# A six-layer cross network on one core: how the first group of x0 reaches TensorE, and who issues two small loads

## The chip, the core and the metric

The kernel runs on one core of a Trainium2 chip. The core has a matrix engine (TensorE, PE in the profile; its weight loads are listed as PEld), a vector engine (VectorE, DVE), a scalar engine (ScalarE, ACT), a general engine (GpSimd, POOL) and a synchronisation engine (SyncE, SP). Data comes from the chip's main memory by DMA; SP, ACT and GpSimd each can issue DMAs on a queue of their own. TensorE writes to the accumulation memory PSUM, which DVE and ACT read.

The metric is device time in microseconds (us), lower is better. "A us at 12.14" below means 12.14 us after the start of the profiled span.

## The reference

Six layers of a cross network, with B = 4096 rows, D = 416 columns, all in bf16:

```python
B, F, D, L = 4096, 26, 16, 6
Din = min(F * D, 1024)                 # 416
x0: (B, Din)   ws: (L, Din, Din)   bs: (L, Din)

def reference(x0, ws, bs):
    x = x0
    for l in range(ws.shape[0]):
        x = x0 * (x @ ws[l] + bs[l]) + x
    return x
```

## The kernel before

The kernel keeps x transposed on the core: columns of x on the 128 partitions, rows along the free axis. The 416 columns are three full planes of 128 (`NK = 3`) and a remainder of 32 (`R`). The planes are in `XM[0]` (x0) and `XM[1]`, `XM[2]` (the running x, by turns), the remainder in `XR[0]` to `XR[2]`, with four groups of rows stacked on the 128 partitions. The 4096 rows are two halves (`s`), each of four groups (`g`) of 512 rows (`CW`).

Layer weights are in `WM` (the 384 rows of the planes) and `WR` (the 32 rows of the remainder, four times on the partitions); `WD` is a block layout of the remainder-by-remainder weights, filled by GpSimd (`fill_wd`, L131). Biases arrive as rows in `bsb` and are transposed on TensorE into `bM` and `bR` (`bias_setup`, L146).

**The head.** SP issues transposing loads, one for each `(s, g)`, which bring 512 rows by 384 columns of x0 from memory straight into `XM[0]` (`load_x0t`, L76): first `(0,0)` and `(0,1)`, then WR of layer 0 (L88), then `(0,2)`, `(0,3)`, `(1,0)`, the remainder columns of s=1 (`xrem`, L85), and the last three of s=1; then the later layers' weights. ACT issues WM of layer 0 (L72), `bsb` (L102) and four loads of the remainder columns of s=0 into `xrig` (L81). ACT and GpSimd then copy WR's 32 rows to the other three strips (L110, L112). While nothing has landed, TensorE runs filler matmuls on a constant tile (`pe_filler`, L141: two of 256 columns, eight of 512, and one more of 512 that the built kernel puts with the others).

**The first layer** (`first_layer`, L208) for s=0: nine matmuls of g=0 (three output planes `m` by three input planes `k`, L214), four transposes of `xrig` (`x0_rem`, L157) whose result DVE copies to `XR[0]` and, with the strips exchanged, to `XRd` (L160); nine matmuls of g=1; eight row matmuls that add the remainder's share (L221); then g=2 and g=3 of each output plane, four more row matmuls, the remainder outputs (`mm_rem`: four of WD at L193, twelve of WM at L198) and the four transposes of s=1's remainder. ACT adds the bias out of PSUM (L165), DVE multiplies by x0 (L166) and adds x (L169). The same follows for s=1, without the transposes.

**Middle layers** run over pairs of tiles `(s, m)` (L181, L187), and **the last layer** swaps the operands, so that it comes out as plain rows, which SP stores.

Engines take their own instructions in order. Which order they stand in is decided by a scheduler when the kernel is built, except where `tc.keep_in_program_order` pins an instruction. PSUM has four slots of two banks (`tag="ps"`); a new tile waits until the one before it in its slot has been read.

In the built kernel, GpSimd's queue before is: constants, identity, zeroing WD, the WR copy, the four WD copies of layer 0, the copy of `xrem` into `xrig` (L134), the later WD copies.

Of the kernel before, what the change touches and what calls it, by code (L numbers as in the profile page):

```python
# [11 lines left out]
BF16 = mybir.dt.bfloat16  # L12
FP32 = mybir.dt.float32
# [3 lines left out]
def kernel(  # L17
# [7 lines left out]
    nc = tc.nc  # L25
    B, D = x0.shape
    L = ws.shape[0]
    P = 128
    NK = 3
    R = D - NK * P  # L30
    assert R == 32 and B == 4096 and D == 416 and L >= 2
    NS = 2
    NG = 4
    CW = 512
# [5 lines left out]
    big = ctx.enter_context(tc.tile_pool(name="big", bufs=1))  # L40
    tpool = ctx.enter_context(tc.tile_pool(name="tpool", bufs=6))
    opool = ctx.enter_context(tc.tile_pool(name="opool", bufs=10))
    psum = ctx.enter_context(tc.tile_pool(name="psum", bufs=4, space=bass.MemoryType.PSUM))

    x0_v = x0.rearrange("(bt p) d -> p bt d", p=P)
    out_v = out.rearrange("(bt p) d -> p bt d", p=P)

    ident = const.tile([P, P], BF16)
    dz = const.tile([P, 2], FP32)
    warm = const.tile([P, CW], BF16)  # L50
    ones = const.tile([P, P], BF16)
    WM = const.tile([P, L, NK, D], BF16)
    WR = const.tile([P, L, D], BF16)
    WD = const.tile([P, L, NG, R], BF16)
    bsb = const.tile([L, D], BF16)
    bLr = const.tile([P, D], BF16)
    bM = const.tile([P, NK, L], FP32)
    bR = const.tile([P, L], FP32)
    X0rows = big.tile([P, NBT, D], BF16)
    XLrows = big.tile([P, NBT, D], BF16)  # L60
    scrR = [big.tile([P, 4, P], BF16, name=f"scrR{s}") for s in range(NS)]
    xrem = big.tile([P, 16, R], BF16)
    xrig = big.tile([P, NS, 4, P], BF16)
    XRd = big.tile([P, NS * CW], BF16)
    XM = [big.tile([P, NK, B], BF16, name=f"XM{i}") for i in range(3)]
    XR = [big.tile([P, NS * CW], BF16, name=f"XR{i}") for i in range(3)]

    def col0(s, g):
        return SW * s + CW * g

    def load_wm(eng, l):
        eng.dma_start(WM[:, l], ws[l, 0:NK * P, :].rearrange("(k p) n -> p k n", p=P))  # L72

    def load_x0t(s, g):
        c0 = col0(s, g)
        nc.sync.dma_start_transpose(out=XM[0][:, :, c0:c0 + CW], in_=x0[c0:c0 + CW, 0:NK * P])  # L76

    def load_xrem0():
        with nc.allow_non_contiguous_dma(reason="64B row segments"):
            for i in range(4):  # L80
                nc.scalar.dma_start(xrig[:, 0, i, :].rearrange("p (g r) -> p g r", g=NG), x0_v[:, i:16:4, NK * P:D])  # L81

    def load_xrem1():
        with nc.allow_non_contiguous_dma(reason="64B row segments"):
            nc.sync.dma_start(xrem[:], x0_v[:, 16:32, NK * P:D])  # L85

    def load_wr0():
        nc.sync.dma_start(WR[0:R, 0, :], ws[0, NK * P:D, :])  # L88

    def load_wr(eng, g, l0, l1):  # L90
        eng.dma_start(WR[32 * g:32 * g + 32, l0:l1, :], ws[l0:l1, NK * P:D, :].rearrange("l r n -> r l n"))
# [2 lines left out]
        nc.vector.memset(warm[:, 2 * P * a:2 * P * a + 2 * P], 0.5)  # L94
    nc.vector.memset(dz[:], 0.0)
    make_identity(nc, ident[:])
    nc.gpsimd.memset(ones[:], 1.0)
    nc.gpsimd.memset(WD[:], 0.0)

    load_x0t(0, 0)  # L100
    load_wm(nc.scalar, 0)
    nc.scalar.dma_start(bsb[:], bs[:, :])  # L102
    load_x0t(0, 1)
    load_xrem0()
    load_wr0()
    nc.scalar.activation(dz[:, 1:2], dz[:, 0:1], ACT.Identity, bias=dz[:, 0:1], scale=1.0)  # L106
    for g in range(1, NG):
        dst, src = WR[32 * g:32 * g + 32, 0, :], WR[0:R, 0, :]
        if g < NG - 1:
            nc.scalar.copy(dst, src)  # L110
        else:
            nc.gpsimd.tensor_copy(dst, src)  # L112
    for g in range(2, NG):
        load_x0t(0, g)
    load_x0t(1, 0)
    load_xrem1()
    for g in range(1, NG):
# [11 lines left out]
    def fill_wd(l0, l1):  # L129
        for g in range(NG):  # L130
            nc.gpsimd.tensor_copy(WD[32 * g:32 * g + 32, l0:l1, g, :], WR[32 * g:32 * g + 32, l0:l1, NK * P:D])  # L131

    fill_wd(0, 1)
    nc.gpsimd.tensor_copy(xrig[:, 1].rearrange("p i (g r) -> p i g r", g=NG), xrem[:].rearrange("p (g i) r -> p i g r", g=NG))  # L134
    fill_wd(1, L)

    wps = psum.tile([P, CW], FP32, tag="ps", name="wps")

    def pe_filler(n, cols):
        for i in range(n):  # L140
            nc.tensor.matmul(wps[:, 0:cols], lhsT=warm[:, 0:P], rhs=warm[:, 0:cols], start=True, stop=True)  # L141

    pe_filler(2, 2 * P)
    pe_filler(8, CW)

    def bias_setup():  # L146
        pb = psum.tile([P, 4, 8], BF16, tag="ps", name="pb")
        for m in range(NK):
            nc.tensor.transpose(pb[:, m, 0:L], bsb[0:L, 128 * m:128 * m + 128], ident[0:L, 0:L])
        for g in range(NG):  # L150
            nc.tensor.transpose(pb[32 * g:32 * g + 32, 3, 0:L], bsb[0:L, NK * P:D], ident[0:L, 0:L], tile_position=(0, 32 * g))  # L151
        nc.vector.tensor_copy(bM[:], pb[:, 0:NK, 0:L])  # L152
        nc.vector.tensor_copy(bR[:], pb[:, 3, 0:L])

    def x0_rem(s, tpr):
        for i in range(4):
            nc.tensor.transpose(tpr[:, 128 * i:128 * i + 128], xrig[:, s, i, :], ident[:])  # L157
        for dst, src in ((slice(0, P), slice(0, P)), (slice(64, P), slice(0, 64)), (slice(0, 64), slice(64, P))):
            to = XR[0] if dst == src else XRd
            nc.vector.tensor_copy(to[dst, CW * s:CW * s + CW], tpr[src])  # L160

    def ew_main(l, s, m, h, pt, cur, nxt, pin=False):
        c0 = col0(s, 2 * h)
        t = tpool.tile([P, 2 * CW], BF16, name="t")
        nc.scalar.activation(t[:], pt[:].rearrange("p a b -> p (a b)"), ACT.Identity, bias=bM[:, m, l:l + 1], scale=1.0)  # L165
        prod = nc.vector.tensor_tensor(out=t[:], in0=t[:], in1=XM[0][:, m, c0:c0 + 2 * CW], op=ALU.mult)  # L166
        if pin:
            tc.keep_in_program_order(prod)
        nc.vector.tensor_tensor(out=nxt[:, m, c0:c0 + 2 * CW], in0=t[:], in1=cur[:, m, c0:c0 + 2 * CW], op=ALU.add)  # L169
# [21 lines left out]
    def mm_rem(l, s, pr, cur, curR):  # L191
        for g in range(NG):
            nc.tensor.matmul(pr[32 * g:32 * g + 32, :], lhsT=WD[:, l, g, :], rhs=curR[:, CW * s:CW * s + CW],  # L193
                             start=True, stop=False, tile_position=(0, 32 * g))
        for k in range(NK):
            for g in range(NG):
                c0 = col0(s, g)
                nc.tensor.matmul(pr[32 * g:32 * g + 32, :], lhsT=WM[:, l, k, NK * P:D], rhs=cur[:, k, c0:c0 + CW],  # L198
                      start=False, stop=(k == NK - 1), tile_position=(0, 32 * g))
# [8 lines left out]
    def first_layer(s):  # L208
        cur, curR, nxt, nxtR = XM[0], XR[0], XM[1], XR[1]

        def full(pt, m, h, gl, after_row):
            c0 = col0(s, 2 * h + gl)
            for k in range(NK):
                nc.tensor.matmul(pt[:, gl, :], lhsT=WM[:, 0, k, 128 * m:128 * m + 128], rhs=cur[:, k, c0:c0 + CW],  # L214
                                 start=(k == 0 and not after_row), stop=(k == NK - 1 and after_row))

        def row(pt, m, h, opens):
            for gl in range(2):
                rg = 32 * ((2 * h + gl) ^ (2 if m == 1 else 0))
                src = XRd if m == 1 else curR  # L220
                nc.tensor.matmul(pt[:, gl, :], lhsT=WR[rg:rg + 32, 0, 128 * m:128 * m + 128],  # L221
                                 rhs=src[rg:rg + 32, CW * s:CW * s + CW],
                                 start=opens, stop=not opens, tile_position=(rg, 0))

        def ph(m):
            return psum.tile([P, 2, CW], FP32, tag="ps", name=f"ph{m}")

        pa = [ph(m) for m in range(NK)]
        if s == 0:
            for m in range(NK):  # L230
                full(pa[m], m, 0, 0, False)
            tp0 = psum.tile([P, CW], BF16, tag="ps", name="tpr")
            x0_rem(0, tp0[:])
            for m in range(NK):
                full(pa[m], m, 0, 1, False)
        else:
            for m in range(NK):
                for gl in range(2):
                    full(pa[m], m, 0, gl, False)
        pb = [ph(0)]  # L240
        row(pa[0], 0, 0, False)
        row(pb[0], 0, 1, True)
        row(pa[2], 2, 0, False)
        row(pa[1], 1, 0, False)
        for m in range(NK):
            ew_main(0, s, m, 0, pa[m], cur, nxt)
        for m in range(NK):
            if m:
                pb.append(ph(m))
            for gl in range(2):  # L250
                full(pb[m], m, 1, gl, m == 0)
        row(pb[1], 1, 1, False)
        row(pb[2], 2, 1, False)
        pr = psum.tile([P, 2, CW], FP32, tag="ps", name="pr")
        mm_rem(0, s, pr[:, 0, :], cur, curR)
        if s == 0:
            x0_rem(1, pr[:, 1, :].bitcast(BF16)[:, 0:CW])
        for m in range(NK):
            ew_main(0, s, m, 1, pb[m], cur, nxt, pin=(s == 0))
        ew_rem(0, s, pr[:, 0, :], curR, nxtR)  # L260

    bias_setup()
    pe_filler(1, CW)
    for s in range(NS):
        first_layer(s)

# [14 lines left out]
    cur, curR = XM[1], XR[1]  # L281
    for l in range(1, LL):
# [30 lines left out]
        cur, curR = nxt, nxtR  # L313

    l = LL
# [97 lines left out]
```

## Time and profile before

| What | Value |
|---|---|
| Median of 3 runs | 130.95 us (130.82 to 131.1) |
| The profiled execution's own time | 130.71 us |
| Its span | 128.9 us |
| TensorE clock granted in it | 0.998 |
| Read from memory / written | 6.15 MB / 3.41 MB |
| SP's transposing loads of x0 | 8, median 4.9 us from issue to landing |
| xrig's four loads on ACT | 32 KB each, median 4.1 us |
| xrem's load on SP | 128 KB, 4.3 us |

Times in the profile come from one execution; the span runs from the first to the last instruction, and the run's time is 1.8 us longer. The row below gives the busy share of the DMA engines in 40 equal slices of 3.2 us, in tenths:

```profile
DMA  3999999999990000000000000000297999995754
```

So the loads fill the first 12 slices, the turning of x back into rows and the stores fill the last dozen. The page also names the costliest groups: line, engine, operation, output and inputs, count | busy us, mean ns | idle before. Three of them, which show what the middle of the kernel is made of:

```profile
L181 PE MATMUL pt<-XM,WM 128*32 128x512 bf16 x1152 | 65.2, 379 | 0.0
L165 ACT ACTIVATE t<-pt,bM 128x1024 bf16<-128x1024 f32 x48 | 49.6, 1115 | 18.3 <-PE pt L187 18.3
L166 DVE TENSOR_TENSOR t<-t,XM 128x1024 bf16<-128x1024 bf16 x60 | 41.4, 690 | 5.3 <-ACT t L165 5.3
```

A matmul's 379 ns is the time from its start to its modelled end; they overlap, so their count times their pitch, not times 379 ns, is the time that TensorE needs.

### The profile page before, as it was taken

Reading aid. Unit: us, or ns where it says so; the run is one execution under the profiler, and the core shown is the slowest. Engines: PE = TensorE matmul, PEld = TensorE weight load, DVE = VectorE, ACT = ScalarE, POOL = GpSimd, SP = SyncE. Lnnn points to the kernel's source line nnn. Section 1 sums busy time; section 2 is a strip of 40 time slices with the busy share of each in tenths; the row PEclk is TensorE's granted clock in tenths of the full one; section 3 lists DMA queues with packets and bytes.
Section 4 is the critical chain, followed back from the end, with each engine's and each line's share of the span. In section 5 each row is a group of like instructions: output and inputs, shape, how many; then the busy total and the mean of one; then the engine's idle time right before and its main releaser. Section 6 shows DMA issues by size and latency. Waiting matters only on the chain.

```text
span 128.9 us, 3973 instructions
## 1 busy us (share of the span) xinstructions
PE 123.1 (96%) x1690; PEld 54.9 (43%) x1690; DVE 107.1 (83%) x197; ACT 86.9 (67%) x99; POOL 5.9 (5%) x18
## 2 busy tenths in 40 slices
PE   6999999999999999999999999999999999999960
PEld 2343443354444444444444444444444445445420
DVE  1032979999999898989898989898989899898991
ACT  0426783987848577848668848668847896569670
POOL 4022200600000000000000000000000000000000
PEclk9999999999999999999999999999999999999999
DMA  3999999999990000000000000000297999995754
GB/s 106 237 203 217 170 158 260 247 328 333 336 299 11 5 0 8 0 0 5 0 5 0 5 0 5 0 5 0 42 166 164 123 219 178 187 323 188 231 179 139
DMA packets 42102, 16.37 MB, mean 127 GB/s; under 512 B 30906, under 2 KB 42084, under 8 KB 42084
## 3 DMA queue, kind: packets, MB, share of 16 engines
q1 hardware_dynamic: 39416, 15.56, 54.6%
q10 hardware_dynamic: 2668, 0.56, 2.3%
q8 instruction: 13, 0.21, 0.7%
q14 instruction: 5, 0.04, 0.1%
HBM read 6.15 MB, written 3.41 MB: 74 GB/s over the span
## 4 chain that ended last, share of the span: by engine, by line
PE 80%; DMA 8%; DVE 5%; issue 2%; SPq 1%; ACT 1%; DVEq 0%
PE pt L181 49%; PE ph L214 9%; DMA XM<-in_x_dram 8%; PE py L327 8%; PE pt L187 5%; PE pr L198 5%; DVE t L355 3%; DVE o L344 2%; PE pr L193 2%; SPq L76 1%; PE py L333 1%; PE ph L221 1%; PE py L336 1%; ACT t L354 1%; PE pr L157 0%
## 5 line engine op out<-in xcount | busy, mean ns | idle before, releaser
L181 PE MATMUL pt<-XM,WM 128*32 128x512 bf16 x1152 | 65.2, 379 | 0.0
L165 ACT ACTIVATE t<-pt,bM 128x1024 bf16<-128x1024 f32 x48 | 49.6, 1115 | 18.3 <-PE pt L187 18.3
L166 DVE TENSOR_TENSOR t<-t,XM 128x1024 bf16<-128x1024 bf16 x60 | 41.4, 690 | 5.3 <-ACT t L165 5.3
L169 DVE TENSOR_TENSOR XM<-t,XM 128x1024 bf16<-128x1024 bf16 x60 | 41.8, 696 | 3.4
L181 PEld LDWEIGHTS <-WM 128*32 128x32 bf16 x1152 | 29.7, 97 | 33.8 <-issue 5.1
L354 ACT CAST t<-py 128x416 bf16<-128x416 f32 (+1 forms) x23 | 14.8, 642 | 4.8 <-PE py L327 2.1
L327 PE MATMUL py<-WM,XM 128*128 128x416 bf16 x96 | 17.7, 340 | 0.0
L214 PE MATMUL ph<-XM,WM 128*128 128x512 bf16 x72 | 16.5, 379 | 0.1
L165 ACT ACTIVATE t<-ph,bM 128x1024 bf16<-128x1024 f32 x12 | 12.5, 1114 | 4.4 <-PE ph L221 4.4
L327 PEld LDWEIGHTS <-XM 128*128 128x128 bf16 x96 | 9.0, 98 | 8.5 <-issue 1.4
L355 DVE TENSOR_TENSOR t<-t,X0rows 128x416 bf16<-128x416 bf16 (+1 forms) x23 | 10.4, 454 | 1.2 <-ACT t L354 1.2
L214 PEld LDWEIGHTS <-WM 128*128 128x128 bf16 x72 | 6.8, 98 | 8.6 <-issue 1.3
L344 DVE TENSOR_TENSOR o<-t,XLrows 128x416 bf16<-128x416 bf16 (+1 forms) x23 | 10.3, 451 | 0.0
L173 ACT ACTIVATE t<-pr,bR 128x512 bf16<-128x512 f32 x10 | 6.4, 684 | 2.7 <-PE pr L198 2.1
L198 PE MATMUL pr<-XM,WM 128*32 128x512 bf16 x120 | 8.2, 379 | 0.0
L187 PE MATMUL pt<-XR,WR 32*128 32x512 bf16 x96 | 7.3, 379 | 0.0
L141 PE MATMUL wps<-warm 128*128 128x512 bf16 (+1 forms) x11 | 4.4, 593 | 1.2 <-DVE warm L94 1.2
L175 DVE TENSOR_TENSOR XR<-t,XR 128x512 bf16<-128x512 bf16 x10 | 4.2, 423 | 0.7
L198 PEld LDWEIGHTS <-WM 128*32 128x32 bf16 x120 | 3.2, 97 | 3.1
L106 ACT ACT_TABLE_LOAD x1 | 1.3, 1283 | 4.3 <-DMA WM<-in_ws_dram 4.3
L174 DVE TENSOR_TENSOR t<-t,XR 128x512 bf16<-128x512 bf16 x10 | 4.2, 418 | 0.0
L152 DVE CAST bM<-pb 128x18 f32<-128x18 bf16 x1 | 0.2, 177 | 4.6 <-PE pb L151 4.6
(39 smaller groups left out, 33.6 us busy)
## 6 DMA issues: line engine op xcount, KB each, us to landing
X0rows<-in_x_dram SPq DMA_DIRECT2D x4, 832.0 KB, 11.6
out_dram<-o SPq DMA_DIRECT2D x9, 208.0 KB, 2.4
WM<-in_ws_dram SPq DMA_DIRECT2D x5, 312.0 KB
out_dram<-o SPq DMA_DIRECT2D x13, 104.0 KB, 1.7
WR<-in_ws_dram SPq DMA_DIRECT2D x4, 130.0 KB, 4.1
WM<-in_ws_dram ACTq DMA_DIRECT2D x1, 312.0 KB
XM<-in_x_dram SPq DMA_TRANSPOSE x8, 4.9
xrig<-in_x_dram ACTq DMA_DIRECT2D x4, 32.0 KB, 4.1
```

The source lines that it names most:

```text
L165: nc.scalar.activation(t[:], pt[:].rearrange("p a b -> p (a b)"), ACT.Identity, bias=bM[:, m, l:l + 1], scale=1.0)
L166: prod = nc.vector.tensor_tensor(out=t[:], in0=t[:], in1=XM[0][:, m, c0:c0 + 2 * CW], op=ALU.mult)
L169: nc.vector.tensor_tensor(out=nxt[:, m, c0:c0 + 2 * CW], in0=t[:], in1=cur[:, m, c0:c0 + 2 * CW], op=ALU.add)
L173: nc.scalar.activation(tr[:, 0:CW], pr, ACT.Identity, bias=bR[:, l:l + 1], scale=1.0)
L181: nc.tensor.matmul(pts[g // 2][32 * q:32 * q + 32, g % 2, :], lhsT=WM[:, l, k, 128 * m + 32 * q:128 * m + 32 * q + 32], rhs=cur[:, k, c0:c ...
L187: nc.tensor.matmul(pts[g // 2][:, g % 2, :], lhsT=WR[32 * g:32 * g + 32, l, 128 * m:128 * m + 128], rhs=curR[32 * g:32 * g + 32, CW * s:CW ...
L198: nc.tensor.matmul(pr[32 * g:32 * g + 32, :], lhsT=WM[:, l, k, NK * P:D], rhs=cur[:, k, c0:c0 + CW], start=False, stop=(k == NK - 1), tile ...
L214: nc.tensor.matmul(pt[:, gl, :], lhsT=WM[:, 0, k, 128 * m:128 * m + 128], rhs=cur[:, k, c0:c0 + CW], start=(k == 0 and not after_row), sto ...
L327: nc.tensor.matmul(py[:, 0:D], lhsT=cur[:, k, q_cols(q, g)], rhs=WM[:, l, k, :], start=((not closes) and k == 0), stop=(closes and k == NK ...
L344: tc.keep_in_program_order(nc.vector.tensor_tensor(out=o, in0=t, in1=xl, op=ALU.add))
L354: nc.scalar.copy(tv, src)
L355: tc.keep_in_program_order(nc.vector.tensor_tensor(out=tv, in0=tv, in1=X0rows[:, b, :], op=ALU.mult))
```

## The change

The first group of s=0 no longer comes by a transposing load. Its 512 rows are loaded as plain rows, all 416 columns, in two tiles `xg0[0]` and `xg0[1]` of two row blocks of 128: one is the first DMA on SP, the other the first on ACT, ahead of WM. TensorE transposes them, twelve transposes of 128 x 128, into bf16 views of PSUM tiles that are in use anyway (`tg0` and the bank of `ph2`), and DVE copies the three planes to `XM[0]`. The remainder columns of that group go from `xg0` to `xrig` by two GpSimd copies; the four `xrig` loads shrink to the other three groups.

`bsb` and WR of layer 0 are issued by GpSimd behind the identity, in place of ACT and SP. The bias transposes stand behind the twelve, into a corner of `ph1`'s tile; DVE makes `bM` and `bR` between the first and the second plane. The fillers shrink from eleven to eight (two of 256 columns, six of 512) and write to the first output tile. The nine matmuls of g=0 run in another order, and the transposes of `xrig` move in between the first three matmuls of g=1 and the other six.

```diff
+    xg0 = [big.tile([P, 2, D], BF16, name=f"xg0{a}") for a in range(2)]
 def load_xrem0():
-                nc.scalar.dma_start(xrig[:, 0, i, :].rearrange("p (g r) -> p g r", g=NG), x0_v[:, i:16:4, NK * P:D])
+                nc.scalar.dma_start(xrig[:, 0, i, R:P].rearrange("p (g r) -> p g r", g=NG - 1),
+                                    x0_v[:, i + 4:16:4, NK * P:D])
 def load_wr0():
-        nc.sync.dma_start(WR[0:R, 0, :], ws[0, NK * P:D, :])
+        tc.keep_in_program_order(nc.gpsimd.dma_start(WR[0:R, 0, :], ws[0, NK * P:D, :]))
...
     make_identity(nc, ident[:])
+    tc.keep_in_program_order(nc.gpsimd.dma_start(bsb[:], bs[:, :]))
+    load_wr0()
...
-    load_x0t(0, 0)
+    for a, eng in enumerate((nc.sync, nc.scalar)):
+        eng.dma_start(xg0[a][:], x0_v[:, 2 * a:2 * a + 2, :])
     load_wm(nc.scalar, 0)
-    nc.scalar.dma_start(bsb[:], bs[:, :])
     load_x0t(0, 1)
     load_xrem0()
-    load_wr0()
+    load_x0t(0, 2)
...
+    for a in range(2):
+        nc.gpsimd.tensor_copy(xrig[:, 0, 2 * a:2 * a + 2, 0:R], xg0[a][:, :, NK * P:D])
...
-    for g in range(2, NG):
-        load_x0t(0, g)
+    load_x0t(0, 3)
...
-    wps = psum.tile([P, CW], FP32, tag="ps", name="wps")
+    pa0 = [ph(m) for m in range(NK)]
+    tg0 = psum.tile([P, 2, CW], FP32, tag="ps", name="tg0")
+    tgv = tg0[:, 0, :].bitcast(BF16).rearrange("p (b c) -> p b c", b=2)
+    planes = [tgv[:, 0, :]] + [pa0[2][:, 0, :].bitcast(BF16)[:, CW * b:CW * b + CW] for b in range(2)]
+    pb = pa0[1][:, 1, :].bitcast(BF16)[:, 0:32].rearrange("p (m l) -> p m l", m=4)
...
     pe_filler(2, 2 * P)
-    pe_filler(8, CW)
+    pe_filler(6, CW)
+    for k in range(NK):
+        for i in range(4):
+            tc.keep_in_program_order(nc.tensor.transpose(planes[k][:, 128 * i:128 * i + 128],
+                                                         xg0[i // 2][:, i % 2, 128 * k:128 * k + 128], ident[:]))
+    bias_setup()
+    for k in range(NK):
+        tc.keep_in_program_order(nc.vector.tensor_copy(XM[0][:, k, 0:CW], planes[k]))
+        if k == 0:
+            tc.keep_in_program_order(nc.vector.tensor_copy(bM[:], pb[:, 0:NK, 0:L]))
+            tc.keep_in_program_order(nc.vector.tensor_copy(bR[:], pb[:, 3, 0:L]))
...
         if s == 0:
-            for m in range(NK):
-                full(pa[m], m, 0, 0, False)
-            tp0 = psum.tile([P, CW], BF16, tag="ps", name="tpr")
-            x0_rem(0, tp0[:])
+            for m, k in ((0, 0), (1, 0), (0, 1), (1, 1), (2, 0), (2, 1), (0, 2), (1, 2), (2, 2)):
+                full(pa[m], m, 0, 0, False, (k,))
             for m in range(NK):
                 full(pa[m], m, 0, 1, False)
+                if m == 0:
+                    x0_rem(0, tgv[:, 1, :])
...
-    bias_setup()
-    pe_filler(1, CW)
```

The copy of `xrem` into `xrig` on GpSimd, the matmuls of g=0 and g=1 and the transposes of `xrig` are pinned in program order now. In the built kernel the lines move: the twelve transposes are L167, the bias transposes L158 and L160, the plane copies L171, the first layer's matmuls L237, the WD matmuls L216, the WM ones behind them L221. GpSimd's queue in it is: constants, identity, the issues of `bsb` and WR, zeroing WD, the two copies from `xg0`, the WR copy, two of the four WD copies of layer 0, the copy of `xrem`, the other two WD copies, the later ones. SP's queue is: the half of `xg0`, transposing loads `(0,1)`, `(0,2)`, `(0,3)`, `(1,0)`, `xrem`, `(1,1)`, `(1,2)`, `(1,3)`, and the weights as before.

## The prediction

> **What bounds the kernel now.** I read the page first, then the chain of waits for the first 36 us, then the timeline of the first 17 us engine by engine. The page says that TensorE is busy almost throughout:
>
> ```profile
> PE 123.1 (96%) x1690; PEld 54.9 (43%) x1690; DVE 107.1 (83%) x197; ACT 86.9 (67%) x99; POOL 5.9 (5%) x18
> ```
>
> The chain of waits (start us, length us, what) shows where it is not TensorE that decides:
>
> ```profile
> 0.74 4.86 DMA XM<-in_x_dram
> 5.59 0.02 issue
> 5.61 1.44 SPq L76
> 7.10 5.00 DMA XM<-in_x_dram
> 12.10 0.04 issue
> 12.14 3.40 PE ph L214 x15
> 15.54 0.33 PE ph L221 x4
> 15.87 0.33 PE pr L193 x4
> 16.20 0.65 PE pr L198 x12
> 16.85 0.33 PE pr L157 x4
> 17.18 3.88 PE ph L214 x18
> ```
>
> Up to 12.14 us the transposing loads of x0 set the pace; the fourth (s=0, g=3) lands at 12.1 and lets the matmul at 12.14 go. From there the chain is TensorE, piece after piece, to 115.8. So what counts is how much earlier TensorE passes 12.14 (first g=3 matmul), 16.20 (first L198) and 17.18 (start of s=1); from there a shift should reach the end unshrunk. The last s=0 sum of layer 0 on DVE starts at 23.57 and layer 1 reads it at 26.9, so DVE is no new bound.
>
> The timeline (start, length, engine, line) shows what fills the first 16 us:
>
> ```profile
> 1.19 4.45 PE L141 MATMUL wps<-warm 128*128 128x256 bf16 x11 [1.19 <-DVE warm L94]
> ...
> 5.57 0.23 PE L149 MATMUL pb<-ident,bsb 6*128 6x6 bf16 x3
> ...
> 5.84 2.12 PE L214 MATMUL ph<-XM,WM 128*128 128x512 bf16 x9
> 5.96 0.18 DVE L152 CAST bM<-pb 128x18 f32<-128x18 bf16 x1 [4.55 <-PE pb L151]
> 6.06 0.16 DVE L153 CAST bR<-pb 128x6 f32<-128x6 bf16 x1
> ...
> 7.80 0.81 PE L157 MATMUL tpr<-ident,xrig 128*128 128x128 bf16 x4
> ...
> 8.62 2.10 PE L214 MATMUL ph<-XM,WM 128*128 128x512 bf16 x9
> 8.64 0.42 DVE L160 COPY XR<-tpr 128x512 bf16<-128x512 bf16 x1 [2.43 <-PE tpr L157]
> ...
> 9.52 0.99 POOL L131 COPY WD<-WR 32x32 bf16<-32x32 bf16 x4
> ...
> 15.26 0.79 POOL L134 COPY xrig<-xrem 128x512 bf16<-128x512 bf16 x1 [4.76 <-DMA xrem<-in_x_dram]
> ```
>
> Real work starts at 5.84. Between there and 12.14 TensorE has 9 matmuls (1.95, one per 0.216), 4 transposes (0.33, by the chain's piece at 16.85), 9 matmuls (1.95), 8 row matmuls (0.54, 10.66 to 11.20) and 3 matmuls (0.65): 5.42 us, taking 6.30. The 0.88 of stall is 0.49 at the xrig loads (0.82 from 7.80 to 8.62, against 0.33) and 0.28 to 0.39 for the fourth transposing load.
>
> **The change, part by part.**
>
> *Loads.* One transposing load leaves the front of SP's queue and two plain halves of 213 KB (128 x 2 x 416 x 2 bytes) come in, one first on SP, one first on ACT ahead of WM. A transposing load costs the rings 2.16 us: three issues ran from 11.45 to 17.93, SP busy all the time. The plain pair, 426 KB at the 314 GB/s of the stretch 2.5 to 3.0 us, takes 1.36. xrig's loads shrink by a quarter; in before the four drained from 3.9 to 8.4 beside transposes, so a quarter of half of that is at most 0.5; I take 0.2. All that follows on SP (g=3 and xrem) is then due 2.16 - 1.36 + 0.2 = 1.0 earlier: g=3 at 11.1, xrem at 14.2 instead of 15.2. Bounds: 0 (the bytes up to g=3 are as many as before, about 2,050 KB, if all move at one rate) and 2.0 (SP reaches xrem's issue that much sooner: one issue of 2.16 and WR's 0.57 and a wait of 0.27 go, two thirds of a us comes in; if issue set the pace).
>
> *First group on TensorE.* The halves land at 3.1 to 3.9: the first from the 2.4 us of a 208 KB store after issue at 0.74, the second from WM's 312 KB, which had landed when the fourth xrig issue went at 3.94. The fillers hold TensorE longer: 1.19 + 2 x 0.213 + 6 x 0.427 = 4.18 (0.427 apart by the weight loads at 3.72, 4.15 and 4.57), so the landing costs nothing up to 4.18 and then one for one. Twelve transposes are added. Warm, 0.083 each (0.33 / 4); before the clock rises, a weight load took 0.15 instead of 0.097, so 0.128 each; a full halving would give 0.166. Fillers were still 0.427 apart at 4.57 and matmuls 0.216 at 5.84, so I put the rise at 5.4: nine and a half at 0.128, the rest at 0.083, end 5.6 (bounds 5.2 and 6.2). Seven bias transposes, 0.27 (5.57 to 5.84), end 5.87.
>
> *Biases by GpSimd.* bsb's issue moves behind the identity, at 1.45. No row shows a load issued there. Bounds: 1.7 from issue to landing (the fastest store) gives 3.2; bsb's own 4.37 on ACT gives 5.8. It no longer stands behind WM, so I take 5.0, which the twelve transposes hide until 5.6; at 5.8 it costs 0.2. The Trainium skill, DMA: Bandwidth & Descriptors, Anatomy of one DMA, fits such a load at 2.0 us plus bytes; that would be an estimate of 3.5, hidden too, and no row of before can test it. WR's issue moves from 4.77 on SP to about 2.5 here, and it needs to be there by 9: hidden. ACT's queue loses bsb's issue (0.70).
>
> *Copies on DVE.* Added: three of 0.42, 0.46 apart with their gap (L160 row). The first hides under the transposes. The other two stand behind bM and bR, which wait for the biases: 5.93 to 6.19, then k=1 to 6.61 and k=2 to 7.07. The matmuls wait here: m0 and m1 of k=0 at 5.87, k=1 from 6.66, and m=2, whose bank holds two planes, from 7.12; five remain, end 8.20 (before 7.80). WM, now behind 213 KB on its ring, must be there by 5.87. It lasted 2.0 beside a transpose (1.9 to 3.94); after the pair, at 3.1, that gives 5.2: hidden.
>
> *To the gate.* Three matmuls, xrig's transposes, six, rows and three more are 3.47: 11.67. xrig's fourth load is issued at the same time as before, 3.9, and landed at 8.37; it is now wanted after 8.85, not 8.05: the 0.49 stall goes. g=3 (11.1) is there. Row matmuls into the next bank wait for DVE's copies of the remainder, 1.34 after xrig's transposes (9.2 + 1.3 = 10.5, wanted at 10.6): no stall, 0.1 to spare. So TensorE passes g=3 at 11.67: 0.47 earlier.
>
> *GpSimd.* Two copies of xg's last columns into xrig are added; between 0.2 (a WD copy) and 0.79 (the xrem copy) each, they start when the halves land, 3.9 at the latest, and are wanted at 8.85: hidden, and so are WR's copies behind them. The order of the built kernel puts the xrem copy (0.79) ahead of two of the four WD copies (0.25 each), which came at 9.5 to 10.5 before. L193 needs all four, and is due at 15.87 - 0.47 = 15.40. With xrem at 14.2: copy to 15.05, WD to 15.55, two of the four L193 matmuls then 0.15, so L198 at 15.75. TensorE's own time for it is 16.20 - 0.47 = 15.73. The two limits meet; I take 0.45 earlier.
>
> The sum is 0.45 off the profiled execution's 130.71 (span 128.9 plus 1.8 around it), which itself lies 0.24 under the median of 130.95. The forecast is 130.95 - 0.45 = **130.5**.
>
> **Rivals.**
>
> *Everything on time.* Transposes warm at 5.2, biases early: bR at 5.8, the nine done by 7.8, g=3 at 11.2, and xrem at 13.6 or sooner so that GpSimd is done by 15.0. Gain 0.95, time 130.0. For it: SP reaches xrem's issue up to 2 us sooner. Against: the rings are full throughout, so loads are paced by draining.
>
> *xrem and GpSimd take the place of the wait (slower).* L198 now starts no sooner than 1.55 after xrem lands (0.85 to the copy's end, 0.5 for WD, 0.2 to L198); before, it needed nothing of xrem. It costs nothing until xrem lands later than 14.2; it turns into a loss when xrem lands after 14.65 (16.20 - 1.55). If the rings move the same bytes at one rate, xrem stays near 15.0, L198 goes at 16.55 and the time is 131.3. For: the byte count. Against: 314 GB/s for plain loads beside 180 for transposing ones (393 KB in 2.16).
>
> *The clock rises late.* The trace has TensorE at half speed past 4.57 while only fillers ran, and the change puts transposes where fillers 7 to 9 ran. If these do not keep the clock rising, the first matmuls run at 0.427 for perhaps one more stretch as long as the first, 5.4 to 8.8: about 3 us at half speed, 1.5 lost, of which 0.6 lies under the DVE waits above. g=3 at 12.6, 0.45 late, 131.4. Against: TensorE has no gap before the clock's rise, and 3 us of fillers stay. The Trainium skill, TensorE: Matmul & The Clock Gate, Part 4, speaks for it: transposes do not engage the fast clock as matmuls do. No row of before has transposes ahead of the rise, so the trace leaves this open.
>
> *The biases land late.* All from bM on shifts with bsb's landing beyond 5.6 (the end of the twelve transposes); at 6.5, g=3 comes at 12.6 again: 131.4. For it: bsb took 4.37 behind one queue's traffic before. Against: an issue at 1.45 with nothing ahead of it.
>
> **Chances.** Forecast 0.48 (own range 130.1 to 130.75); all on time 0.14; xrem 0.16; clock 0.14; biases 0.08. 0.2% is 0.26 us, about what a measurement of this kernel can tell from no change. Faster: 0.40 of the forecast and 0.13 of the first rival, with 0.01 of others, 0.54. Same: 0.07 of the forecast, 0.06 of xrem, and 0.03 of the rest, 0.16. Slower: 0.30. The range reaches from 129.8, a little past the first rival, to 131.4, where the slower ones lie.
>
> **What would show it.** Right: first L237 matmul near 5.9, with a wait for DVE of about half a us after the second; the first g=3 matmul at 11.5 to 11.8; TensorE's wait in L216 under 0.2. Wrong: transposes starting after 4.3 (halves late); L158 waiting for bsb; L237 matmuls 0.427 apart after 6; xrem landing after 14.6 with TensorE waiting for WD. Also if a shift at 17 us does not reach the end.

## The result, and the profile after

The changed kernel is slower. Median 132.31 us (131.68 to 132.61, six executions) against 130.88 (130.66 to 131.1, six) for the kernel before on the same chip: ratio 1.0093, 95% interval 1.0069 to 1.0117, a loss of 1.43 us. The forecast was 130.5, its range 129.8 to 131.4. The execution profiled first took 131.68, span 129.9 (before: 130.71 and 128.9). It is the quickest of the six, so its trace shows only some 1.0 us of the loss; e13 to e15 below are for the rest. In this document medians and ranges take in every execution, while ratios leave out the slow ones, those over 1.5% above the fastest of the same kernel (two each in e2, e4 and e10, one each in e7 and e8).

Its page, first part (busy us, share of the span, instructions), reads almost as before: TensorE has 0.2 us and nine instructions more.

```profile
PE 123.3 (95%) x1699; PEld 55.9 (43%) x1699; DVE 108.3 (83%) x200; ACT 86.9 (67%) x99; POOL 8.7 (7%) x22
```

The chain of waits of the changed kernel (start, length, what) is no longer paced by transposing loads but by the biases:

```profile
1.47 5.02 DMA bsb<-in_bs_dram
...
6.87 0.32 PE ph L237
...
7.23 2.65 PE ph L237 x11
...
11.39 0.81 PE ph L246 x8
12.20 3.99 PE ph L237 x18
...
16.52 0.55 PE pr L216 x4
17.07 0.65 PE pr L221 x12
...
18.05 3.88 PE ph L237 x18
```

`bsb` is issued at 1.47 and lands 5.02 us later, at 6.49. Everything real on TensorE stands behind it. The same points before and after:

| Point | Before | Forecast | After | After - before |
|---|---|---|---|---|
| First real matmul, s=0 g=0 | 5.84 | 5.87 | 6.81 | +0.97 |
| First g=2 matmul (row matmuls done) | 11.20 | 11.02 | 12.14 | +0.94 |
| First of the twelve WM matmuls of the remainder | 16.20 | 15.75 | 17.07 | +0.87 |
| Start of s=1 | 17.18 | 16.73 | 18.05 | +0.87 |
| Layer 1 | 26.90 | 26.45 | 27.77 | +0.87 |
| Span | 128.9 | 128.45 | 129.9 | +1.0 |

(The first two rows are from the timelines, where a piece can start a little before the one ahead of it ends: 12.14 there is 12.20 in the chain. The forecasts of the last four are the recorded gain of 0.45 off before, 11.02 is the recorded 11.67 less three matmuls of 0.216.) The shift is there almost whole at the first matmul and runs to the end.

The timeline of the changed kernel (start, length, engine, line, operation; in brackets the idle time before it and what ended it) shows the parts of the change:

```profile
4.58 1.06 PE L167 MATMUL ph<-ident,xg 128*128 128x128 bf16 x8
...
6.54 0.22 PE L158 MATMUL ph<-ident,bsb 6*128 6x6 bf16 x3 [0.89 <-DMA bsb<-in_bs_dram]
...
7.02 0.15 DVE L174 CAST bR<-ph 128x6 f32<-128x6 bf16 x1
7.09 0.75 DVE L171 COPY XM<-ph 128x512 bf16<-128x512 bf16 x2
7.23 0.10 PEld L237 LDWEIGHTS <-WM 128*128 128x128 bf16 x1 [0.31 <-issue]
...
14.78 0.61 POOL L139 COPY xrig<-xrem 128x512 bf16<-128x512 bf16 x1 [5.63 <-DMA xrem<-in_x_dram]
...
15.46 1.17 POOL L136 COPY WD<-WR 32x32 bf16<-32x32 bf16 x2
```

The transposes start when the fillers end (4.16) and are done at 5.64, where 5.6 was forecast. Then TensorE stands for 0.89 us with nothing ahead of the bias transposes in its queue, and DVE's second and third plane copies wait with it (7.09). The second matmul's weight load (7.23) comes 0.06 after DVE's copy of `bR` ends (7.17); it is 0.05 to 0.06 in e3, e4, e6, e7 and e13 to e15 too. So this matmul, whose output tile also holds the transposed biases, seems to wait for that copy; the profile names no cause. GpSimd's copy of `xrem` starts at 14.78, and the two WD copies behind it take 1.17 together and end at 16.63: the four L216 matmuls take 0.55 instead of 0.33.

### The profile page after: what moved, and what is told of

It is laid out like the page before. It is cut to its first block, busy times and chain, and to the rows that moved or that the text cites. A ratio compares the mean times of both kernels' runs of the same rounds, so it can differ in the third digit from the quotient of the medians.

```text
span 129.9 us, 4000 instructions
## 1 busy us (share of the span) xinstructions
PE 123.3 (95%) x1699; PEld 55.9 (43%) x1699; DVE 108.3 (83%) x200; ACT 86.9 (67%) x99; POOL 8.7 (7%) x22
## 4 chain that ended last, share of the span: by engine, by line
PE 82%; DVE 7%; DMA 6%; issue 2%; ACT 1%; POOL 0%; DVEq 0%; POOLq 0%
PE pt L204 49%; PE ph L237 12%; PE py L347 5%; PE pt L210 5%; PE pr L221 5%; DVE t L375 4%; DMA bsb<-in_bs_dram 4%; DVE o L364 3%; PE pr L216 2%; DMA out_dram<-o 2%; PE ph L246 2%; PE py L353 1%; ACT t L374 1%; PE py L356 1%; PE pr L178 0%
## 5 line engine op out<-in xcount | busy, mean ns | idle before, releaser
L237 PE MATMUL ph<-XM,WM 128*128 128x512 bf16 x72 | 16.7, 379 | 0.0
L237 PEld LDWEIGHTS <-WM 128*128 128x128 bf16 x72 | 6.7, 98 | 8.5 <-issue 1.4
L364 DVE TENSOR_TENSOR o<-t,XLrows 128x416 bf16<-128x416 bf16 (+1 forms) x23 | 10.3, 453 | 0.0
L221 PE MATMUL pr<-XM,WM 128*32 128x512 bf16 x120 | 8.4, 379 | 0.0
L136 POOL COPY WD<-WR 32x32 bf16<-32x32 bf16 (+1 forms) x8 | 4.3, 537 | 7.6 <-DMA WR<-in_ws_dram 7.2
L221 PEld LDWEIGHTS <-WM 128*32 128x32 bf16 x120 | 3.2, 97 | 3.0
L152 PE MATMUL ph<-warm 128*128 128x512 bf16 (+1 forms) x8 | 3.2, 578 | 1.2 <-DVE warm L96 1.2
```

Of the source, the lines that this page charges most:

```text
L237: mm = nc.tensor.matmul(pt[:, gl, :], lhsT=WM[:, 0, k, 128 * m:128 * m + 128], rhs=cur[:, k, c0:c0 + CW], start=(k == 0 and not after_row) ...
L364: tc.keep_in_program_order(nc.vector.tensor_tensor(out=o, in0=t, in1=xl, op=ALU.add))
```

## The experiments

Where an edit is shown, it is made to the changed kernel, unless said otherwise. The kernel before on the same chip took 130.94 us beside e1 to e4 (16 executions), 131.06 beside e5 to e8 (30) and 130.98 beside e9 to e12 (26).

**e13 to e15: the changed kernel as it is, three more executions**, one time each: 133.4, 132.98 and 131.46 us, beside 130.56 for the kernel before.

> The changed kernel once more, unchanged, for a trace of an execution near its median of 132.3 (the one traced so far took 131.68, its lowest). Half-speed theory: in an execution of 132.2 or more the biases land at 6.4 to 7.4, TensorE stands idle more than 0.9 us before the bias transposes, and at least three of the first twelve real matmuls have weight loads 0.42 apart rather than 0.216, so that the stretch from the first of them to the fourth matmul group (12.20 in the first trace) is 0.3 us or more longer. Rival, late loads only: all matmuls but the first two or three 0.216 apart, and the extra 0.6 us is a later landing of the biases or of xrig's fourth load.

> As the run before it: another execution of the changed kernel, the same two expectations. If it takes less than 131.9, its first matmuls are at full speed from the fourth on by both theories.

> As the two before it: another execution of the changed kernel, the same two expectations.

They ask what the rest of the median is made of. The biases landed at 6.65, 6.33 and 5.91. In the last, the first matmul starts at 6.25 and the start of s=1 is 0.61 late. The first two are the ones to look at. The timeline of the 133.4 us execution, weight loads only (one for each matmul; what counts is the distance between starts):

```profile
3.96 0.82 PEld L167 LDWEIGHTS <-xg 128*128 128x128 bf16 x12 [0.50 <-DMA xg<-in_x_dram]
6.69 0.13 PEld L158 LDWEIGHTS <-bsb 6*128 6x128 bf16 x3 [1.91 <-DMA bsb<-in_bs_dram]
...
7.77 0.15 PEld L237 LDWEIGHTS <-WM 128*128 128x128 bf16 x1 [0.27 <-issue]
8.19 0.15 PEld L237 LDWEIGHTS <-WM 128*128 128x128 bf16 x1 [0.28 <-issue]
```

and its stretches (us, length, busy time of PE, PEld, DVE, ACT, POOL with counts, granted clock, DMA share, GB/s):

```profile
6.40:8.00 1.60, 1.27 (x10) 0.60 (x11) 0.91 (x4) 0.00 (x0) 0.00 (x0) 0.78 1.43 158
8.00:9.60 1.60, 1.60 (x5) 0.57 (x4) 0.00 (x0) 1.07 (x2) 0.94 (x3) 0.50 1.34 247
9.60:11.20 1.60, 1.60 (x7) 0.54 (x6) 0.00 (x0) 0.00 (x0) 0.00 (x0) 0.65 1.13 203
```

Here the transposes run at full speed at once (twelve weight loads in 0.82 us), so the idle time before the biases is longer: 1.74 us on TensorE. The granted clock then falls to 0.50 from about 7.3 to 10.7 (1.6 us at a mean of 0.78, then 0.50, then 0.65), and eight matmuls run 0.427 apart: the eleven matmuls of the chain's piece at 7.23 above take 4.16 instead of 2.65. The 132.98 us execution reads the same (landing at 6.33, 1.47 idle, clock 0.50, 4.31 for the eleven). In the executions of 131.68 and 131.46 the granted clock is 1.00 throughout this stretch and the eleven or twelve take 2.65 and 3.01. So the half-speed expectation holds for executions well above the median, though it is not a later landing that tells them apart: 6.33 in the 132.98 us one is earlier than 6.49 in the 131.68 us one, and below the 6.4 that was expected. What does tell the four apart is when the clock rose: in the two longer ones it was up before the transposes, whose weight loads take 98 ns, in the other two not yet (151 ns). Those between 132.2 and 132.6 were not traced; that a shorter piece at half speed makes them is inferred.

The Trainium skill, TensorE: Matmul & The Clock Gate, Part 1, describes a gate that halves the clock after an idle window of about 3.4 us and doubles it after a busy one, the windows running freely, whatever the kernel does. The trace agrees in the length of the low stretch (3.4 us, 7.3 to 10.7) and in what free windows lead one to expect, that the same kernel is caught in one execution and not in another. It differs in that 1.5 to 1.7 us without work were enough here.

**e1: the biases taken off the path of the first matmuls.**

```diff
-    bias_setup()
     for k in range(NK):
         tc.keep_in_program_order(nc.vector.tensor_copy(XM[0][:, k, 0:CW], planes[k]))
-        if k == 0:
-            tc.keep_in_program_order(nc.vector.tensor_copy(bM[:], pb[:, 0:NK, 0:L]))
-            tc.keep_in_program_order(nc.vector.tensor_copy(bR[:], pb[:, 3, 0:L]))
+
+    def bias_late():
+        bias_setup()
+        tc.keep_in_program_order(nc.vector.tensor_copy(bM[:], pb[:, 0:NK, 0:L]))
+        tc.keep_in_program_order(nc.vector.tensor_copy(bR[:], pb[:, 3, 0:L]))
...
                 full(pa[m], m, 0, 0, False, (k,))
+            bias_late()
```

> The bias transposes and the making of bM and bR move behind the nine matmuls of g=0; the biases are still issued by GpSimd. Theory (the biases' late landing at 6.5 holds TensorE): the nine matmuls start when WM is there, about 6.05, and end near 8.0 instead of 9.3; the first g=2 matmul comes about 0.8 to 1.0 earlier than the changed kernel's 12.2; the time falls to about 130.9 to 131.3, on which the WD wait (L216) then takes back some 0.3. Rival (clock: the changed kernel's loss is a TensorE clock that falls in the gap before the biases): the gap shrinks as well, so the time falls too, but first of all the spread of the runs, 131.7 to 132.6, shrinks to a tenth or two. Rival (xrem and GpSimd set the time): no gain, L198 stays near 17.0.

132.02 us (131.16 to 132.58), ratio 1.008 (1.0051 to 1.0109). The first real matmul starts at 5.43 instead of 6.81, so it was the biases that held it. Yet the time is hardly lower than the changed kernel's, and the spread is no smaller. In the profiled execution (132.5) three things eat the gain: matmuls 0.43 apart until 7.0, though TensorE has no gap ahead of them, a wait for `xrig`'s fourth load (9.86), and this, from its chain of waits:

```profile
10.45 4.58 DMA xrem<-in_x_dram
...
15.14 0.98 POOL xrig L139
...
16.78 0.68 POOL WD L136
...
17.90 0.65 PE pr L222 x12
```

The last WD copy ends at 17.46, 2.4 us after `xrem` landed, where I had booked 1.35. The twelve matmuls start at 17.90, 1.70 later than before the change.

**e2: `bsb` on ACT's queue between the half of `xg0` and WM.**

```diff
-    tc.keep_in_program_order(nc.gpsimd.dma_start(bsb[:], bs[:, :]))
...
+    nc.scalar.dma_start(bsb[:], bs[:, :])
     load_wm(nc.scalar, 0)
```

> Only the biases' load goes back to ACT's queue, between the half of xg and WM. Theory (it is GpSimd's issue that is slow): the biases land at about 4.5, the bias transposes follow the twelve without a wait, and the first matmul waits for WM at 6.1 to 6.5 (its issue moves 0.5 back); time 131.0 to 131.6. Rival (any small load takes 5 us beside this traffic, whoever issues it): the biases land near 6.2 again and the time stays within 0.3 of the changed kernel's.

135.65 us (134.65 to 136.72), ratio 1.033 (1.0295 to 1.0364). The biases are there in time, their transposes run at 5.35. But WM, issued 0.67 us later than in the changed kernel and behind `bsb` on its queue, lands at 9.51; the chain of the execution profiled (136.68):

```profile
1.92 7.59 DMA WM<-in_ws_dram
...
9.56 5.30 PE ph L237 x12
```

Twelve matmuls of 0.216 take 5.30 behind 3.87 us of idle time, with a granted clock of 0.50. A far worse loss by the same two steps: a late load, then the clock.

**e3: the four WD copies of layer 0 pinned ahead of the copy of `xrem`.**

```diff
-            nc.gpsimd.tensor_copy(WD[32 * g:32 * g + 32, l0:l1, g, :], WR[32 * g:32 * g + 32, l0:l1, NK * P:D])
+            cp = nc.gpsimd.tensor_copy(WD[32 * g:32 * g + 32, l0:l1, g, :], WR[32 * g:32 * g + 32, l0:l1, NK * P:D])
+            if l0 == 0:
+                tc.keep_in_program_order(cp)
```

> Only the order on GpSimd changes: all four WD copies of layer 0 stand ahead of the xrem copy. Theory (biases): TensorE's wait of 0.22 in L216 goes, nothing else; time 0.2 lower than the changed kernel's. Rival (xrem and GpSimd set the time): 0.9 lower, as fast as before.

132.88 us (131.19 to 133.15), ratio 1.0113 (1.0065 to 1.016): two groups, 131.2 to 131.5 and 132.8 to 133.15. The WD wait is gone (four matmuls 0.33). In the profiled execution, 133.15, the biases land at 7.07 and the twelve matmuls take 4.10, half speed until 10.3. The granted clock reads 1.00 all the while, and the weight loads take 0.15 before the gap of 1.48 as well as behind it: here the clock has not fallen, it has not risen yet (as in e10). So GpSimd's order is worth 0.2 in the chain; the times (132.88 against 132.31) are too scattered to show it, and the scatter of the head does not depend on it.

**e4: the gap bridged with three fillers of 256 columns ahead of the bias transposes.**

```diff
+    for i in range(3):
+        tc.keep_in_program_order(nc.tensor.matmul(pa0[0][:, 0, 0:2 * P], lhsT=warm[:, 0:P], rhs=warm[:, 0:2 * P], start=True, stop=True))
     bias_setup()
```

> Three filler matmuls of 256 columns (0.64 us at the low clock) are added between the twelve transposes and the bias transposes, so that TensorE has no gap of 0.9 there. Clock rival: the first matmul of g=0, 0.42 apart from the second in the changed kernel, is at full speed, and the slower runs (132.2 to 132.6) go; median near 131.7 or below. Theory (biases): biases land as before and the profiled execution stays within 0.2 of 131.7; the spread stays.

131.88 us (131.29 to 134.06), ratio 1.0072 (1.0047 to 1.0097). The bridge is too short: in the execution profiled (134.06) the fillers run at full speed at 5.27, the biases land at 7.36, TensorE waits 1.59, and the granted clock falls to 0.50 at 8.6 and comes back at 12.0. The transposes' weight loads shorten from 151 to 97 ns between 5.0 and 5.2, so the clock rose there, fell 3.4 us later and came back 3.4 us after that. Whether a bridge that lasts to the landing keeps the clock up was not tried, as it delays the bias transposes themselves.

**e5: e1 and e3 together**, so no bias ahead of the first matmuls and no WD behind `xrem`.

> Bias transposes behind the nine matmuls, as in the first experiment, and all WD copies of layer 0 ahead of the xrem copy, as in the third. If in the first experiment GpSimd's late WD took what the biases gave back (L217 waited to 17.5), the waits add up: L222 at about 16.9 instead of 17.9, time 0.6 to 1.0 under the first experiment's 132.0, about 131.2. If only the clock counts, no gain over the first experiment.

131.23 us (130.94 to 132.31), ratio 1.0024 (1.0005 to 1.0043). Most of the loss is gone, but no gain appears. The start of s=1 is at 17.41, against 17.18 before. The weight load of the last `xrig` transpose waits 0.47 for `xrig`'s fourth load (issued 4.22, landed 9.40) and the row matmuls take 0.81.

**e6: GpSimd issues `bsb` and WR ahead of the identity instead of behind it.**

```diff
+    tc.keep_in_program_order(nc.gpsimd.dma_start(bsb[:], bs[:, :]))
+    load_wr0()
     make_identity(nc, ident[:])
-    tc.keep_in_program_order(nc.gpsimd.dma_start(bsb[:], bs[:, :]))
-    load_wr0()
```

> GpSimd issues the biases and WR at 0.74, before it makes the identity and before SP's first transposing load (1.25); the built order then has WD ahead of xrem as well. Theory (a small load behind the first transposing load waits for it, whoever issues it): the biases land before 5.4, the first matmul goes at 5.4 to 5.7 with WM there, and the time falls to 130.7 to 131.3. Rival (GpSimd's issue takes 5 us by itself): the biases land at about 5.9 and the first matmul goes near 6.2, time 131.4 to 131.8.

131.38 us (131.02 to 132.63), ratio 1.0033 (1.0013 to 1.0053). The issue comes only 0.21 us earlier (1.26 against 1.47), beside SP's first transposing load and not ahead of it as expected, so what standing ahead of that load would do is not shown:

```profile
1.26 0.66 POOL L98 DMA_DIRECT2D bsb<-in_bs_dram  x1 [0.81 <-POOLq L417]
```

The load takes 4.1 us in this execution, the bias transposes come at 5.57 and the first matmul at 5.87, the forecast's time to the hundredth. (The built order also has the WD copies ahead of `xrem` here, worth 0.2 in e3's chain.) From the chain:

```profile
4.19 5.41 DMA xrig<-in_x_dram
...
11.17 0.81 PE ph L246 x8
11.98 3.99 PE ph L237 x18
```

So with the biases in time the forecast's start is met, and the forecast's 11.02 for g=2 is still missed by 0.89 (11.91 in the timeline): the fourth `xrig` load lands at 9.60, the rows take 0.81 rather than 0.54, and the first matmuls are 0.41 to 0.42 apart until 7.1.

**e7: nine fillers of 512 instead of six.**

```diff
-    pe_filler(6, CW)
+    pe_filler(9, CW)
```

> Nine fillers of 512 columns instead of six, ahead of the twelve transposes; these then start at about 5.5 and end near 6.6, about when the biases land anyway. Clock theory (the low clock comes from the idle stretch before the biases, since it rises and falls by how busy TensorE was): the nine matmuls of g=0 are all 0.216 apart, and the slow end of the runs (132.2 and more) goes; median 131.5 to 131.9. If the clock is not the cause of the spread: median 132.2 to 132.6, the transposes being 0.2 later.

132.01 us (131.19 to 134.21), ratio 1.0058 (1.0035 to 1.0082). The transposes move to 5.20 and end at 6.03, the biases still land at 6.50, and the chain is the changed kernel's within 0.02 us. An idle 0.52 is left. Filling the time does not help while the load is late, and against the clock theory the long end of the times stays (132.21 and 134.21).

**e8: the kernel before, with only the two issues moved to GpSimd** (GpSimd's copies pinned in the order they have before).

```diff
     make_identity(nc, ident[:])
+    tc.keep_in_program_order(nc.gpsimd.dma_start(bsb[:], bs[:, :]))
+    load_wr0()
...
-    nc.scalar.dma_start(bsb[:], bs[:, :])
     load_x0t(0, 1)
     load_xrem0()
-    load_wr0()
```

> The kernel before with one part of the change alone: the biases and WR of layer 0 issued by GpSimd behind the identity. Theory (it is this issue, behind the transposing loads already queued, that makes the biases late): they land at 6.3 to 7.4 instead of 5.56, the first L214 matmul moves from 5.84 to 6.6 or later, and the time goes up by 0.6 to 1.2 to about 131.8. Rival (the lateness comes from the plain halves ahead of them): they land near 5, no change, 130.9.

131.13 us (130.82 to 132.9), ratio 1.0036 (0.9997 to 1.0074). Seven executions lie at 130.82 to 131.17, five at 132.58 to 132.9. The chain of one of the seven (130.84):

```profile
1.48 4.65 DMA bsb<-in_bs_dram
...
6.51 2.05 PE ph L216 x9
...
11.30 3.99 PE ph L216 x18
```

So the biases are late (6.12) without plain halves ahead of them. In the timeline the first matmul comes 0.60 later than before (6.44 against 5.84), and the 18 matmuls of g=2 and g=3 only 0.04 later (11.24 against 11.20), with no stall at the fourth transposing load, and the start of s=1 is at 16.93, earlier than before's 17.18. So 0.6 us of lateness in the first matmul was hidden by the stalls that stand behind it in the kernel before (0.88 in the prediction), and the loss of 0.6 to 1.2 that was expected is not there in these seven. The five upper executions lie 1.8 above; nine matmuls at half speed would cost 9 x 0.211 = 1.9. That this is their cause is inferred from e10, not traced here.

**e9: e1, e3 and e6 together.**

> The three edits that helped, together: biases issued by GpSimd ahead of the identity, bias transposes behind the nine matmuls of g=0, WD ahead of xrem. If the biases still cost anything where they stand in the fifth experiment: 0.1 to 0.3 under its 131.2. Theory by now: xrig's fourth load, which landed at 9.4 to 9.9 in experiments 1, 5 and 6 and held TensorE for 0.5, is the limit that is left: the first g=2 matmul again near 11.8, time 131.1 to 131.3, no faster than before.

131.54 us (131.0 to 131.9), ratio 1.004 (1.0019 to 1.0061). In the profiled execution (131.9) WM is now late (its first weight load waits 0.62, to 5.93), `xrig`'s fourth load lands at 10.18 (a weight load waits 0.81), and g=2 starts at 12.56.

**e10: e9 with both halves of `xg0` on SP**, so that ACT starts with WM.

```diff
-    for a, eng in enumerate((nc.sync, nc.scalar)):
+    for a, eng in enumerate((nc.sync, nc.sync)):
```

> As the run named e9, but both halves of xg are issued by SP, and ACT begins with WM and xrig as in the kernel before. If xrig's late fourth load comes from standing behind xg and WM on ACT's ring: it lands near 8.5, no wait, the first g=2 matmul near 11.2, time 130.5 to 130.9, though the halves land some 0.3 later. If DMA traffic as a whole sets xrig: 9.4 again, 131.1 to 131.3.

131.88 us (131.05 to 133.25), ratio 1.0061 (1.0023 to 1.0098): six executions at 131.05 to 131.19, six at 132.56 to 133.25. The one profiled is from the upper group:

```profile
1.25 4.29 DMA xg<-in_x_dram
...
6.83 3.80 PE ph L240 x9
```

The second half lands at 5.54, TensorE idles 1.01 (timeline) between two transposes, and the nine matmuls take 3.80 instead of 1.95: 1.85 lost, about as much as lies between the groups. TensorE turns to `xrig` only at 11.3 here, so this trace can't show whether its fourth load lands near 8.5, as expected. The lower group is no faster than the kernel before (130.98). The granted clock reads 1.00 here, as it does under the fillers from 1.19 to 4.16, which are 0.427 apart too: a clock that has not risen yet does not show in that row, only one that fell again (e4, e13). The distance between weight loads shows both.

**e11: e9 with nine fillers** (the edit of e7).

> As e9, with nine fillers of 512 columns instead of six: the transposes start at about 5.2 at full speed, the nine matmuls go from 6.1 with the clock up. Clock theory: the median is as in e9 or better by 0.1, since the half-speed stretch after the first matmul goes, and the runs spread less. If the start of the real work counts: 0.3 to 0.6 slower than e9.

131.74 us (131.34 to 131.96), ratio 1.0062 (1.0039 to 1.0085). With no gap, fillers to transposes to matmuls, the nine take 2.12 at full speed and six executions lie within 0.62 us. But the matmuls start at 6.51, and rows still take 0.81. The scatter is a little smaller than e9's (0.9 over nine executions), and there is no gain.

**e12: e9 with two of `xrig`'s four loads issued by SP ahead of the first transposing load.**

```diff
-            for i in range(4):
+            for i in range(2):
...
+    with nc.allow_non_contiguous_dma(reason="64B row segments"):
+        for i in range(2, 4):
+            nc.sync.dma_start(xrig[:, 0, i, R:P].rearrange("p (g r) -> p g r", g=NG - 1), x0_v[:, i + 4:16:4, NK * P:D])
     load_x0t(0, 1)
```

> As e9, with two of xrig's four loads issued by SP between its half of xg and the first transposing load; no xrig load waits for a free semaphore now. If xrig's fourth load is the limit: TensorE no longer waits for it, the first g=2 matmul comes near 11.2, time 130.5 to 130.9, faster than before. If the transposing loads, pushed back by about 1 us, are the limit: TensorE waits for g=1 or g=3 instead, 131.2 or more.

131.33 us (130.99 to 131.98), ratio 1.0032 (1.0013 to 1.005). The wait for `xrig` is gone, but the first matmuls are 0.39 to 0.43 apart until 6.9 and g=2 starts at 11.63, not near 11.2. What is late next, from the chain:

```profile
11.15 7.18 DMA XM<-in_x_dram
```

A transposing load of s=1 lands at 18.33 and holds TensorE for 0.4. It was issued at 11.15, no later than before (11.45) and 0.11 later than in the changed kernel (11.04), so the two issues did not push it back; why it takes 7.18 us is not shown. Layer 1 starts at 27.61, against 26.90 before.

No version of the changed kernel is faster than the kernel before; the nearest is e5, whose interval for the ratio, 1.0005 to 1.0043, still lies above 1.

## Why the prediction was wrong

*The step that failed* is the term "Biases by GpSimd ... I take 5.0, which the twelve transposes hide until 5.6; at 5.8 it costs 0.2". The biases landed at 6.49, 6.65, 6.33 and 5.91 in four traced executions of the changed kernel and at 7.07 and 7.36 in e3 and e4: 4.4 to 5.9 us after the issue, where I had 3.55 and bounds of 1.75 to 4.35. The upper bound was wrongly made. I took 4.37, `bsb`'s own duration on ACT, as the slowest, because I thought it spent that behind WM; but in e8 the load took 4.65 with nothing ahead of it on its queue. So the bound was one load's own time in one execution, and no bound at all. And I costed the lateness only up to the bound, although the bias transposes stand ahead of all real matmuls on TensorE and `bM` and `bR` ahead of two plane copies on DVE, so that each 0.1 counts.

*The mechanism* was written down as the fourth rival, "The biases land late", with "at 6.5, g=3 comes at 12.6 again: 131.4", and given 0.08. It measured 6.49, g=3 at about 12.85, 131.68.

*The sum against the first profiled execution.* The forecast had the start of s=1 at 16.73, it came at 18.05: 1.32 later. Of it 0.94 is the first matmul (6.81 for 5.87). 0.27 is "Row matmuls ... no stall, 0.1 to spare": the eight took 0.81 for 0.54, in the changed kernel and in every variant, also where they came at 10.98 (e5); they wait on DVE's three remainder copies, which end 1.35 us after the `xrig` transposes (10.10 to 11.45) as I had worked out, while the rows behind the six matmuls are due after 1.29. 0.14 is GpSimd: the copies of `xrem` came 0.6 us after my time (14.78 for 14.2), and the two WD copies took 1.17 for 0.5. These make 1.35, of which 0.03 was regained elsewhere. The last 0.1 to 1.42 comes behind layer 1.

*The clock*, my third rival at 0.14, was right in kind: e14 and e13 lie 1.3 and 1.7 over the first profiled execution, and I infer that the 0.63 by which the median lies over it has the same cause. I looked for that cause in the transposes. The runs show half speed behind a gap: a clock that had risen falls (e13, e14, e4), or one that had not risen stays low (e3, and e10 with its gap between transposes). Whether transposes in the place of fillers also delay the rise stays open. Without a gap the matmuls of e11 are at full speed from the first, with nine fillers, but those of e5 and e1, with six, are 0.30 to 0.43 apart until 6.2 and 7.0.

*What held.* The halves landed early enough (transposes at 4.16, forecast 4.18), and the transposes were done when I said (5.64 for 5.6; 0.107 apart and not 0.128 then 0.083). WM was there in time in the changed kernel (in e1 the first matmul runs at 5.43), though not in e9 and e12 (5.93 and 5.67). The wait for DVE was there, but in two parts: the second matmul comes 0.42 after the first, the third 0.33 after the second. The third comes 0.75 after the first, forecast 0.79. The fourth transposing load no longer stalls. The shift at 17 us reached the end.

*What the gain was worth.* With the biases in time (e5, e6, e9, e12) the ratio falls from 1.0093 to between 1.0024 and 1.004: some 60 to 75% of the loss is gone, but there is no gain. (With the wait the gap goes as well, so how much of this is the clock's is not separated.) I had `xrig`'s fourth load "issued at the same time as before", landing at 8.37 and wanted at 8.85. It landed at 9.40 to 10.18 in e1, e5, e6 and e9, since its issue waits for a half of `xg0` (e5: landed 4.20, issue 4.22; before it was 3.94) and the load then takes 5.2 to 5.9 us. So the stall of 0.49 that I struck out stays, and 0.27 of row wait is new: these two are the 0.45 of the forecast and more. When `xrig` is mended (e12), a load of s=1 is late. My reading is that the head is bound by what the DMA engines bring in 12 us, and that the change reorders it without making it less, which the prediction had as its lower bound for the loads (gain 0); no run here tests that by itself.

*Still open:* why a 5 KB load takes 4.1 to 5.9 us here, and what sets its value from one execution to the next.

## What to carry to other kernels

Before a small load is put on another queue, ask what stands behind it on its consumer's queue, and cost its landing with the slowest load of its size in the same traffic, not with the quickest; if a late landing holds a whole engine, move its consumer back first (e1's edit) and the load second. A gap of 1 to 2 us soon after TensorE's clock has risen, or before it has, can cost twice: the gap, and in some executions another 1.1 to 1.9 us of matmuls at half speed (e3, e4, e10, e13, e14); a kernel whose times fall in two groups about that far apart should have its weight loads' distances read in the head. And an earlier first matmul is worth only what the stalls behind it do not already absorb: e8 started 0.60 later than before and lost nothing in its lower group.

## What the runs showed of the hardware that was not expected

- A load of 4.9 KB took 4.37 us on ACT's queue before and at most 4.1 in e2, and on GpSimd's 4.65 in e8 and 4.1 to 5.9 in the changed kernel and its variants. How much of this is the queue's and how much the traffic's is not separated. The Trainium skill, DMA: Bandwidth & Descriptors, Anatomy of one DMA, fits a load issued by GpSimd at 2.0 us and its bytes; every such landing traced here is at over twice that.
- WM's 312 KB, issued at 1.92 instead of 1.25 behind a transposing load issued at 1.25, and behind `bsb` on its own queue, landed at 9.51 instead of before 5.4 (e2; e1 for the latter): 0.67 us of issue became some 4 us of landing.
- TensorE's clock fell to half behind 1.5 to 1.7 us of idle time (e4, e13, e14), 3.4 us after it had risen in e4, and stayed there for 3.4 us of dense matmuls. Behind gaps of 0.89 and 0.52 (the changed kernel, e7) it did not fall.
- The WD copies on GpSimd took 0.25 each before, and 0.55 to 0.68 each when they ran beside DVE's work at 15 to 17 us (e1); in e2 two of them at 16.9, with DVE idle, took 0.23 each.
